# Chunked attention beside matrix products: five pieces per tile, or two turns per tile

## The chip, the cores and the metric

One core of one Trainium2 chip runs the whole program. The metric is the device time of one execution in microseconds (us); less is better. TensorE (PE) does the matrix products, VectorE (DVE), ScalarE (ACT) and GpSimd (POOL) work element by element, and SyncE (SP) issues most of the DMAs.

## The reference, cut to what matters

```python
# attention: 4 batches, 8 heads, 768 rows, 64 columns; chunks of 32 queries
for c in range(nc):
    k_full = concat(mem_k, k[16 rows before the chunk .. 8 rows after it])
    v_full = concat(mem_v, v[the same rows])
    scores = scale * q_c @ k_full.T
    a = exp(scores - max(scores)); a = a / (sum(a) + 1e-9)
    out[chunk] = a @ v_full
x = out as (3072, 512)
h = x @ w_in;  x = (h * tanh(softplus(h))) @ w_out
xn = x / rms(x) * rms_g
return (silu(xn @ w_gate) * (xn @ w_val)) @ w_out2
```

All inputs are float32. The kernel splits each operand of a large product into a high and a low part and adds three products of the parts.

## The kernel before, in words

The 3072 rows are worked in four batches of 768. A batch has six attention tiles of 128 rows (`TPP` is 6). The first batch's attention runs at the start. The attention of batch j (1, 2, 3) runs beside the products with `w_in` of batch j - 1, whose rows are then already there. For batch 1 these products are the units (`unit`, L682), for batches 2 and 3 the groups (`group1`, L714, over `group`, L643: seven products per group by a Strassen-like scheme). A product (`product`, L632) is six matmuls of 128x128 by 384 columns, recorded under L639, L640 and L641. Both `unit` and `group` yield after each product. The stretch from one yield to the next is called a slot. Batch 1 has 52 slots, batches 2 and 3 have 56 each.

At each yield `run` (L699) calls `between` (L998, made by `slots`, L990). It counts the slots in `n`, issues stores that are due, calls attention pieces until their share is done, converts some weights, and from slot `n_slots - 7` on builds the operands T of the next stage out of the new attention rows (`tail_of`, L1022, with its sums at L615 to L618 and splits at L153 and L154).

One attention tile t takes five operations on PE, each followed by work of other engines:

- a (L433): four 128x128 transposes of the queries (L438) and four of the next keys (L395), in one of two rotating PSUM banks each (`bank`, L332). It also issues the loads of later queries and keys. a1 (L445) copies them out on ACT (L449, L408, L409) and DVE (L404). `att_a0` does the first keys of a batch.
- b (L453): the scores, 32 small matmuls of a 64x32 block by 64 columns, into the bank pair `bkp` (L458). A small float32 matmul leaves two records. b1 (L466): DVE takes the maximum and subtracts it (L471, L472), ACT takes the exponential (L477).
- c (L486): four transposes of the probabilities (L490), into a rotating bank. c1 (L495) copies them on ACT (L497).
- d (L501): the values, again 32 small matmuls, into the same bank pair `bkp` (L506). It issues the load of the values of tile t + 2. d1 (L516): DVE forms the sums and multiplies (L519, L520, L522).
- e (L528): four transposes of the result (L532), into a rotating bank. e1 (L535) copies them on ACT (L539).

`att_list(j)` (L544) makes the list for a batch: step s holds e of tile s - 4, d of s - 3, c of s - 2, b of s - 1 and a of s, each with its own follow-up as one piece. That makes 31 pieces with the one of `att_a0`. `between` spreads them evenly: piece number m is called at the first slot n with `m * (n_slots - 7) < n * 31`.

The order in which each engine gets its instructions is set at build time by a planner (`schedule_with_timeline_sim`, L19). It goes by program order as priority, and may put an instruction ahead of, or behind, others if its model of the engines finds them not ready. `pin` keeps the order of some.

Of the kernel before, what the change touches and what calls it, by code (L numbers as in the profile page):

```python
# [29 lines left out]
def tile_kernel(  # L30
# [30 lines left out]
    TPP = 2 * NSUB  # L61
# [45 lines left out]
    def flush(all_=False):  # L107
        tick[0] += 1
        while late and (all_ or late[0][0] <= tick[0]):
            _, dst, src = late.pop(0)  # L110
            nc.sync.dma_start(out=dst, in_=src)
# [197 lines left out]
    def cv_upto(n):  # L309
        while cv_n[0] < n:  # L310
            next(cv[0], None)
            cv_n[0] += 1
# [231 lines left out]
    def att_list(j):  # L544

        out = []
        t0 = TPP * j
        for s in range(TPP + 4):
            for op, lag in (("e", 4), ("d", 3), ("c", 2), ("b", 1), ("a", 0)):
                t = t0 + s - lag  # L550
                if t0 <= t < t0 + TPP:
                    if op == "a" and t % SPB == 0:
                        out.append([(att_a0, t)])
                    out.append([(att_ops[op], t), (att_ops[op + "1"], t)])
        return out


    ttab_x, ttab_n = {}, {}

    def t_new():  # L560
# [2 lines left out]
    def g_new():  # L563
        return gp.tile([128, 2, N], F32, tag="g", name="g")
# [16 lines left out]
    def t_pieces(j, x0, x1, new, temp_new, dram, tab):  # L581

        return sum_pieces(j, x0[:, 0:2, :], x0[:, 2:4, :], x1[:, 0:2, :], x1[:, 2:4, :],
                          new, temp_new, dram, tab)
# [405 lines left out]
    def slots(pieces, conv, tail=(), more={}, cap=10 ** 6):  # L990


        state = dict(n=0, att=0, tail=0)
        plist, n_slots = pieces
        first_cv, to = conv
        base = cv_n[0]

        def between():  # L998
            state["n"] += 1
            n = state["n"]  # L1000
            flush()
            if n in more:
                more[n]()
            span = n_slots - 7
            while state["att"] < len(plist) and state["att"] * span < n * len(plist):
                for fn, t in plist[state["att"]]:
                    fn(t)
                state["att"] += 1
            if n > first_cv:
                cv_upto(min(cap, base + (to - base) * (n - first_cv) // (n_slots - first_cv)))  # L1010
            if n >= n_slots - 7 and tail:
                if state["tail"] == 0:
                    state["t"] = tail()
                    for fn in state["t"][0]:
                        fn()
                elif state["tail"] <= len(state["t"][1]):
                    state["t"][1][state["tail"] - 1]()
                state["tail"] += 1

        return between  # L1020

    def tail_of(j):  # L1022
        return lambda: t_pieces(j, xb.pop(2 * j), xb.pop(2 * j + 1), t_new, lambda p: g_new(), None, ttab_x)

    def keep_w(i, half):
        return lambda: w_store(("i", i), half)
# [5 lines left out]
    CV_I = 64  # L1032

    def then(more, n, fn):
        more.setdefault(n, []).append(fn)

    def finish_at(more, i, n):
        part = finish(("i", i))
        for step in range(3):
            then(more, n + step, lambda: next(part))  # L1040

    def calls(more):
        return {n: (lambda fns=fns: [fn() for fn in fns]) for n, fns in more.items()}

    units = [(1, i) for i in range(NHEAD)]
    units += [(b, i) for i in (3, 4, 7, 5, 6) for b in range(2)]
    at = {u: 4 * n + 4 for n, u in enumerate(units)}
    more = {}
    finish_at(more, 7, at[1, 7] + 1)
    bt = slots((att_list(1), 4 * len(units)), (0, 73), tail_of(1), calls(more), CV_I)  # L1050
    for b, i in units:
        run([unit(b, i)], bt)
    for i in range(3):
        del wtab["i", i]
    more = {}
# [4 lines left out]
        finish_at(more, i, 3 * n + 1)  # L1060
    for n, i in ((8, 2), (15, 1), (22, 0)):
        then(more, n, lambda: None)
    bt = slots((att_list(2), 56), (12, CV_I + 33 + 11), tail_of(2), calls(more), CV_I + 33)
    for i in down:
        group1(1, i, bt)
    more = {}
    for i, ns in ((0, (1, 3)), (1, (8, 10)), (2, (15, 17))):
        for half, n in enumerate(ns):
            then(more, n, keep_w(i, half))
    bt = slots((att_list(3), 56), (0, 0), tail_of(3), calls(more))  # L1070
    for pos, i in enumerate(up):
        group1(2, i, bt)
        reload(pos, up)
# [2 lines left out]
    def late_pool(name, bufs, side="left"):  # L1076
        return ctx.enter_context(tc.tile_pool(name=name, bufs=bufs, side=side, reuse_waits="tile"))
# [1 line left out]
    w2p[0] = late_pool("w2p", 1, "right")  # L1079
    late_pools["s"] = late_pool("gs", 3, "right")  # L1080
    late_pools["gr"] = late_pool("gr", 1, "right")
    bt = slots(([], 56), (0, CV_I + 44))
    for pos, i in enumerate(down[:-1]):
        group1(3, i, bt)
        if 1 <= pos <= 3:
# [41 lines left out]
    for s, (m, i) in enumerate(steps):  # L1127
        t = feed.next(s)
# [57 lines left out]
    def between2(to, n_slots):  # L1186
        state = dict(n=0)
        base = cv_n[0]

        def fn():  # L1190
            flush()
            if pend:
                pend.pop(0)()
                return
            n_raw[0] = 10 ** 6
            state["n"] += 1
            cv_upto(min(to, base + (to - base) * state["n"] // n_slots))

        return fn

    bt = between2(CV_I + 220, 100)
# [13 lines left out]
    units = [(j, r) for j in jback for r in range(NSUB2)]  # L1215
# [17 lines left out]
    bt = between2(CV_I + 298, 92)  # L1233
# [54 lines left out]
```

## Time and profile before

| what | us |
|---|---|
| median of 3 runs | 1166.82 |
| lowest and highest of them | 1164.63, 1167.36 |
| the profiled execution, its own time | 1167.72 |
| its span, from first to last instruction | 1166.0 |

In the timeline a row is a start, a duration, an engine and a line. Matmuls are pipelined, so a duration overlaps the next start. What an operation costs PE is read from the distance between starts. In rows of stretches, each engine has its busy time and its count of instructions, then follow the granted clock of PE as a share of full speed, the busy share of the DMA engines, and GB/s.

### The profile page before, as it was taken

The page shows a single profiled execution, that of the slowest core. Times are in us where ns is not written, and L with a number is a line of the kernel's source. Part 1 is how long each engine was busy: PE and PEld are TensorE (multiplying, and loading weights), DVE is VectorE, ACT ScalarE, POOL GpSimd, SP SyncE. Part 2 cuts the span into 40 slices and gives each one's busy share as a digit, 9 for nine tenths or more (in the row PEclk, how much of TensorE's full clock was granted, in tenths as well). Part 3 has the DMA queues.
Part 4 walks back from the last instruction along what each step waited for, and adds up shares of the span by engine and source line. Part 5 has one row for each costly group of instructions (what it writes and reads, how often), then busy time and mean ns, then how long its engine had stood idle before and what let it go on. Part 6 is the DMA issues. An engine that isn't in the chain of part 4 may idle for free.

```text
span 1166.0 us, 22910 instructions
## 1 busy us (share of the span) xinstructions
PE 1140.7 (98%) x9052; PEld 1005.2 (86%) x9052; DVE 823.8 (71%) x1254; ACT 629.2 (54%) x1008; POOL 183.4 (16%) x165
## 2 busy tenths in 40 slices
PE   5899999999999999999999999999999999999998
PEld 4799999999999888888878778888888888999998
DVE  3655798844745876866776765967896857888873
ACT  4566666543645896677775443544454423444441
POOL 3011231311132311010011121110211111000000
PEclk8899999999999999999999999999999999999999
DMA  9989799898488774594599398999898889655421
GB/s 195 187 219 224 191 300 260 240 297 284 170 302 290 255 225 144 188 354 157 195 375 409 123 349 316 355 407 359 312 363 356 329 283 319 180 160 145 145 91 37
DMA packets 213276, 294.20 MB, mean 252 GB/s; under 512 B 104240, under 2 KB 160560, under 8 KB 204336
## 3 DMA queue, kind: packets, MB, share of 16 engines
q1 hardware_dynamic: 210864, 284.34, 73.5%
q0 software_dynamic: 2304, 8.39, 2.3%
q8 instruction: 71, 1.16, 0.4%
q14 instruction: 37, 0.30, 0.1%
HBM read 181.80 MB, written 110.89 MB: 251 GB/s over the span
## 4 chain that ended last, share of the span: by engine, by line
PE 75%; DMA 9%; DVE 8%; ACT 5%; issue 2%; POOL 0%; SPq 0%; ACTq 0%; DVEq 0%; POOLq 0%
PE bk L639 13%; PE bk L640 13%; PE bk L641 13%; DMA s<-g_scratch 4%; PE bk L912 4%; PE bk L914 4%; PE bk L913 4%; PE bk L755 3%; PE bk L756 3%; PE bk L754 3%; DVE T L154 2%; PE bkp L639 2%; PE bkp L640 2%; PE bkp L641 2%; PE bkp L506 2%
## 5 line engine op out<-in xcount | busy, mean ns | idle before, releaser
L639 PE MATMUL bk<-T,w 128*128 128x384 f32 (+1 forms) x860 | 315.6, 369 | 1.3 <-ACT c L657 1.0
L640 PE MATMUL bk<-T,w 128*128 128x384 f32 (+1 forms) x860 | 311.2, 362 | 0.0
L641 PE MATMUL bk<-T,w 128*128 128x384 f32 (+1 forms) x860 | 307.4, 361 | 0.0
L639 PEld LDWEIGHTS bk<-T,w 128*128 128x128 f32 x860 | 162.0, 189 | 21.0 <-ACT c L657 1.3
L640 PEld LDWEIGHTS bk<-T,w 128*128 128x128 f32 x860 | 161.9, 188 | 16.5 <-DVE T L154 0.3
L641 PEld LDWEIGHTS bk<-T,w 128*128 128x128 f32 x860 | 161.5, 188 | 15.8
L912 PE MATMUL bk<-w,T 128*128 128x256 f32 x396 | 112.1, 283 | 0.2 <-ACT T L153 0.2
L913 PE MATMUL bk<-w,T 128*128 128x256 f32 x396 | 112.0, 283 | 0.0
L914 PE MATMUL bk<-w,T 128*128 128x256 f32 x396 | 111.9, 283 | 0.0
L755 PE MATMUL bk<-T,w 128*128 128x512 f32 x276 | 107.5, 390 | 0.5 <-DVE T L154 0.5
L756 PE MATMUL bk<-T,w 128*128 128x512 f32 x276 | 107.1, 389 | 0.0
L754 PE MATMUL bk<-T,w 128*128 128x512 f32 x276 | 105.8, 389 | 0.0
L669 POOL TENSOR_TENSOR v<-c,v 128x512 f32<-128x512 f32 x36 | 54.1, 1503 | 291.7 <-DVE c L665 259.0
L665 DVE TENSOR_TENSOR c<-bk,c 128x512 f32<-128x512 f32 (+2 forms) x72 | 43.0, 598 | 54.5 <-PE bk L641 41.9
L912 PEld LDWEIGHTS bk<-w,T 128*128 128x128 f32 x396 | 76.0, 192 | 0.5 <-ACT T L153 0.4
L913 PEld LDWEIGHTS bk<-w,T 128*128 128x128 f32 x396 | 76.0, 192 | 0.0
L914 PEld LDWEIGHTS bk<-w,T 128*128 128x128 f32 x396 | 75.9, 192 | 0.0
L649 ACT COPY c<-bk 128x512 f32<-128x512 f32 (+2 forms) x72 | 36.9, 514 | 69.1 <-PE bk L641 25.3
L154 DVE TENSOR_TENSOR T<-s,T 128x1024 fp32r<-128x1024 f32 (+1 forms) x50 | 62.5, 1258 | 15.2 <-ACT T L153 15.1
L782 ACT ACTIVATE s<-s 128x1024 f32<-128x1024 f32 x44 | 46.4, 1059 | 31.3 <-DMA s<-g_scratch 31.2
L755 PEld LDWEIGHTS bk<-T,w 128*128 128x128 f32 x276 | 51.8, 188 | 11.6 <-DVE T L154 0.9
L756 PEld LDWEIGHTS bk<-T,w 128*128 128x128 f32 x276 | 51.8, 188 | 10.8
(228 smaller groups left out, 2284.6 us busy)
## 6 DMA issues: line engine op xcount, KB each, us to landing
T<-nt_scratch SPq DMA_DIRECT2D x35, 1024.0 KB
g_scratch<-g SPq DMA_DIRECT2D x64, 384.0 KB
s<-g_scratch SPq DMA_DIRECT2D x46, 512.0 KB
h_scratch<-s SPq DMA_DIRECT2D x36, 512.0 KB
w<-wg SPq DMA_DIRECT2D x10, 1792.0 KB
wg<-w SPq DMA_DIRECT2D x30, 512.0 KB
raw<-in_moe_w_out_dram SPq DMA_DIRECT2D x28, 512.0 KB
nt_scratch<-T SPq DMA_DIRECT2D x14, 1024.0 KB
```

Of the source, the lines that this page charges most:

```text
L154: keep((eng or nc.vector).tensor_tensor(lo, src, hi.bitcast(F32), op=ALU.subtract))
L639: nc.tensor.matmul(ps, whi, xh, start=first and kk == 0, stop=False, **more)
L640: nc.tensor.matmul(ps, whi, xl, start=False, stop=False, **more)
L641: nc.tensor.matmul(ps, wlo, xh, start=False, stop=kk == 1, **more)
L669: nc.gpsimd.tensor_tensor(c22, u3, z5, op=ALU.add)
L754: nc.tensor.matmul(ps, ahi, bhi, start=start, stop=False)
L755: nc.tensor.matmul(ps, ahi, blo, start=False, stop=False)
L756: nc.tensor.matmul(ps, alo, bhi, start=False, stop=stop)
L782: nc.scalar.activation(x, g, self.act)
L912: nc.tensor.matmul(ps, t[:, 0, f], w[:, 0], start=first and f == 0, stop=False, **more)
L913: nc.tensor.matmul(ps, t[:, 0, f], w[:, 1], start=False, stop=False, **more)
L914: nc.tensor.matmul(ps, t[:, 1, f], w[:, 0], start=False, stop=f == HG - 1, **more)
```

## The change: two turns per tile

The list of pieces is replaced by a list of turns, each with a place on the axis of slots. For step s (0 to 8) the near turn holds b of tile s - 1, a of s, then a1 of s and b1 of s - 1. The far turn, 0.62 of a step later, holds d of s - 2, e of s - 3, c of s - 1, then d1 of s - 2, e1 of s - 3 and c1 of s - 1. A step is `span / 8.62` slots: 5.22 for batch 1 and 5.68 for batches 2 and 3. `att_list` stays in use for batch 0.

```diff
+    def att_turns(j, span):
+
+        t0 = TPP * j
+        out = [(0, [(att_a0, t0)])]
+        for s in range(TPP + 3):
+            near = [(att_b, s - 1), (att_a, s), (att_a1, s), (att_b1, s - 1)]
+            far = [(att_d, s - 2), (att_e, s - 3), (att_c, s - 1), (att_d1, s - 2), (att_e1, s - 3),
+                   (att_c1, s - 1)]
+            for at, ops in ((s, near), (s + 0.62, far)):
+                ops = [(fn, t0 + t) for fn, t in ops if 0 <= t < TPP]
+                if ops:
+                    out.append((at * span / (TPP + 2.62), ops))
+        return out
...
-        plist, n_slots = pieces
+        tiles, n_slots = pieces
+        plist = att_turns(tiles, n_slots - 7) if tiles is not None else []
...
-            span = n_slots - 7
-            while state["att"] < len(plist) and state["att"] * span < n * len(plist):
-                for fn, t in plist[state["att"]]:
+            while state["att"] < len(plist) and plist[state["att"]][0] < n:
+                for fn, t in plist[state["att"]][1]:
                     fn(t)
                 state["att"] += 1
...
-    bt = slots((att_list(1), 4 * len(units)), (0, 73), tail_of(1), calls(more), CV_I)
+    bt = slots((1, 4 * len(units)), (0, 73), tail_of(1), calls(more), CV_I)
...
-    bt = slots((att_list(2), 56), (12, CV_I + 33 + 11), tail_of(2), calls(more), CV_I + 33)
+    bt = slots((2, 56), (12, CV_I + 33 + 11), tail_of(2), calls(more), CV_I + 33)
...
-    bt = slots((att_list(3), 56), (0, 0), tail_of(3), calls(more))
+    bt = slots((3, 56), (0, 0), tail_of(3), calls(more))
...
-    bt = slots(([], 56), (0, CV_I + 44))
+    bt = slots((None, 56), (0, CV_I + 44))
```

## Rows read from the trace of the kernel before

**Rows 1.** The page, busy time of each engine.

```profile
PE 1140.7 (98%) x9052; PEld 1005.2 (86%) x9052; DVE 823.8 (71%) x1254; ACT 629.2 (54%) x1008; POOL 183.4 (16%) x165
```

**Rows 2.** Stretches: start:end, length, busy (count) PE, PEld, DVE, ACT, POOL; clock, DMA, GB/s.

```profile
140.00:180.00 40.00, 40.00 (x536) 36.83 (x535) 39.39 (x70) 27.59 (x54) 11.56 (x14) 1.00 0.97 284
...
226.00:300.10 74.10, 73.92 (x1148) 67.58 (x1147) 36.71 (x74) 29.67 (x57) 8.19 (x8) 1.00 0.87 274
300.10:365.00 64.90, 64.80 (x358) 62.34 (x357) 40.09 (x64) 36.10 (x60) 17.24 (x15) 1.00 0.76 268
```

**Rows 3.** Waits of PE from 60 to 345 us: total, times, longest.

```profile
PE bk L395 <- DVE kw L412: 0.9, 1, 0.9
PE bk L639 <- DVE c L665: 0.2, 1, 0.2
```

**Rows 4.** PE by line, 63.1 to 300.1 us; L641 as L640, L506 as L458.

```profile
L639 PE MATMUL bk<-T,w 128*128 128x384 f32 x319 | 113.0, 355 | 0.2 <-DVE c L665 0.2
L640 PE MATMUL bk<-T,w 128*128 128x384 f32 x318 | 107.9, 339 | 0.0
...
L458 PE MATMUL bkp<-kw,qT 64*32 64x64 f32 x1152 | 17.5, 224 | 0.0
...
L395 PE MATMUL bk<-ident,kn 128*128 128x128 f32 (+1 forms) x76 | 11.8, 266 | 0.0
L490 PE MATMUL bk<-ident,p 128*128 128x128 f32 x72 | 11.2, 278 | 0.0
```

**Rows 5.** Timeline of PE, a d and a c, each alone between products.

```profile
242.91 0.34 PE L641 MATMUL bk<-T,w 128*128 128x384 f32 x1
243.18 0.86 PE L506 MATMUL bkp<-vw,pT 64*32 64x65 f32 x64
...
244.26 0.34 PE L640 MATMUL bk<-T,w 128*128 128x384 f32 x1
...
244.95 0.34 PE L641 MATMUL bk<-T,w 128*128 128x384 f32 x1
...
245.75 0.33 PE L640 MATMUL bk<-T,w 128*128 128x384 f32 x1
245.92 0.33 PE L641 MATMUL bk<-T,w 128*128 128x384 f32 x1
...
247.48 0.34 PE L641 MATMUL bk<-T,w 128*128 128x384 f32 x1
```

**Rows 6.** Timeline of PE, a b with an e right behind it.

```profile
202.35 0.34 PE L641 MATMUL bk<-T,w 128*128 128x384 f32 x1
202.62 0.86 PE L458 MATMUL bkp<-kw,qT 64*32 64x64 f32 x64
203.41 0.66 PE L532 MATMUL bk<-ident,x 128*128 128x128 f32 x4
...
204.08 0.34 PE L640 MATMUL bk<-T,w 128*128 128x384 f32 x1
```

**Rows 7.** Timeline of PE, a b cut by products, first to last part.

```profile
145.21 0.34 PE L639 MATMUL bk<-T,w 128*128 128x384 f32 x1
145.48 0.41 PE L458 MATMUL bkp<-kw,qT 64*32 64x64 f32 x20
...
146.10 0.34 PE L641 MATMUL bk<-T,w 128*128 128x384 f32 x1
...
149.03 0.30 PE L458 MATMUL bkp<-kw,qT 64*32 64x64 f32 x4
```

**Rows 8.** Timeline, a b and a d, and the DVE steps that free `bkp`.

```profile
154.58 0.86 PE L458 MATMUL bkp<-kw,qT 64*32 64x64 f32 x64
...
161.01 0.68 DVE L472 TENSOR_TENSOR p<-bkp,mx 128x512 f32<-128x512 f32 x1
...
186.02 0.86 PE L506 MATMUL bkp<-vw,pT 64*32 64x65 f32 x64
...
189.84 0.68 DVE L522 TENSOR_TENSOR x<-bkp,sm 128x512 f32<-128x512 f32 x1
```

## The prediction

> **What bounds the kernel now.** I read the page first: PE is busy for 98% of the span [rows 1], so the question is what PE does, and whether it ever waits for the attention. The stretches come next. From 140 to 180 us, from 226 to 300 and from 300 to 365, PE is busy for practically all of the time at a granted clock of 1.00 [rows 2]. Then the waits: from 60 to 345 us, where the attention of batches 1 to 3 runs, PE waits only twice, 1.1 us together [rows 3]. So these stages are bound by PE issuing instructions one after the other. A change there can gain by making attention cheaper for PE, and can lose by making PE wait. What is saved passes on, because the stage behind is bound by PE too [rows 2]: its loads, conversions and stores are issued as products advance, so they move along.
>
> **What attention costs PE now.** Between 63.1 and 300.1 us PE does 319 + 318 + 318 = 955 matmuls of products, 1152 records each of scores and values, and 72 or 76 transposes of each of four kinds [rows 4]. One product matmul takes (247.48 - 245.92) / 9 = 0.1733 us from start to start [rows 5]. Thus 955 x 0.1733 = 165.5 us of the 237.0 are products, and 71.5 us are attention.
>
> What would it be if every operation stood alone and whole? A d alone moves a product from 242.91 to 244.26, which is 1.35 us, where two product steps take 0.35: so it costs 1.00 us [rows 5]. A c alone costs 245.75 - 244.95 - 0.35 = 0.45 us [rows 5]. There are 1152 / 64 = 18 b and 18 d, and (3 x 72 + 76) / 4 = 73 sets of four transposes: 36 x 1.00 + 73 x 0.45 = 68.9 us. The kernel pays 71.5, in spite of some neighbours that already save a little. The rest is in bursts cut in parts. One b is cut in four [rows 7]: the part of 20 records costs 146.10 - 145.21 - 0.35 = 0.54 us, where 20/64 of the 0.79 us that a whole burst occupies [rows 6] would be 0.25. A part too many so costs 0.29 us. In the timeline of the three batches I count nine such parts: three in each of the first b of batches 2 and 3, and three single ones. Those first b come right behind a (pieces 1 and 3 of the list, 3.2 slots apart at most), and the planner puts products between the parts that are ready.
>
> **The change, part by part.**
>
> *Neighbours.* A b with an e behind it costs 204.08 - 202.35 - 0.35 = 1.38 us [rows 6], against 1.00 + 0.45 apart: 0.07 saved by the contact of small matmuls with transposes. For contact between two sets of transposes I take nothing. Per batch, the near turns make five such contacts (b with a, s = 1 to 5) and the far turns six (d with e or c, s = 2 to 7). In three batches that is 33 x 0.07 = 2.3 us. Whole turns would cost 68.9 - 2.3 = 66.6 us, against 71.5: **4.9 us less**.
>
> *Cuts.* That sum has no part cut. Bounds: all nine cuts come back (2.6 us lost again) or none. The a of a tile now lies a whole step, 5.68 slots (5.22 in batch 1), ahead of its b, so the two b in four parts should become whole; the single cuts, where the planner fills a hole, can recur anywhere. I take two, 0.6 us.
>
> *The bank pair.* Scores and values share `bkp`, and the two turns are closer than the pieces were. From d to the next b the list had two pieces, 2 x 49/31 = 3.2 slots, with a c between; now there are 0.38 x 5.68 = 2.16 slots, with e and c. At 6 x 0.1733 = 1.04 us a slot that is 2.25 + 0.9 = 3.15 us. From b to the next d it was 4.7 slots; now 0.62 x 5.68 = 3.52 slots and a's 0.9 us, 4.6 us. What DVE needs, in the stretch where it is busy for 39.39 of 40 us [rows 2]: behind the b at 154.58 the subtraction ends at 161.69, 6.25 us after the burst's end; behind the d at 186.02 the multiplication ends at 190.52, 3.64 us after [rows 8]. At those lags PE would wait 1.65 and 0.5 us. From 226 us on DVE is half busy [rows 2], and I see no wait. Bounds: nothing (the planner puts the burst behind products when it expects the lag, as it does now: a lag of 6.25 us and no PE wait in that stretch [rows 3]), up to 6 x (1.65 + 0.5) = 12.9 us for batch 2, all six tiles at the worst rows. A gain is excluded, as there is next to nothing to remove. I am nearest to the row without waits, and take 0.3 us.
>
> *Other engines.* The work of DVE, ACT and POOL is the same in number and shape. In a near turn a1's copies (one on DVE, three on ACT) now stand ahead of b1; behind them wait c and then d, but c comes only after 4.6 us, d and e, and d a full step after c1. In a far turn d1 stands behind e on PE because `x` has one buffer, and e1 goes ahead of c1 on ACT. Each is covered by the slots to the next turn; if that cover goes, the price is the one of the bank pair. The two rotating banks are reused in the order q, k, e, c; between c and the next q lie 2.16 slots and a b, 3.2 us, for two copies on ACT, which is busy for 27.59 of 40 us [rows 2].
>
> *DMAs moved.* SP gets the same DMAs. The loads of v at d(t) are used at d(t + 2), two steps or 11.4 slots later, where the list had 11 at its closest; q likewise 11.4 against 7.9; the keys after a batch's first 5.68 against 4.7. PE waits for no DMA now [rows 3], and the closest distances grow, so I cost them at nothing. If a v load came late, the stores behind it on SP would be late too, and their buffers.
>
> *Ends of batches.* The last e comes at slot 49 (45 in batch 1), in the same call as the sums that need it and ahead of them, one slot later than in the list; but its d is now five slots ahead instead of 1.6, so its x is ready. I cost this at nothing: the seven slots up to the next stage hide the sums and splits, as they do now. If that cover went, the price would be the slot that it is later, 1.04 us.
>
> **Sum.** 4.9 - 0.6 - 0.3 = 4.0 us less: 1167.7 - 4.0 = 1163.7 us against the profiled execution. That lies 0.9 us above the median of the runs, so I predict **1162.8 us**. About 0.3%, 3.5 us, is what a measurement of this kernel can tell from no change, so this is just beyond it.
>
> **A rule against it.** Going from a product to a d takes 0.27 us instead of 0.17, in which the product behind has to drain [rows 5]. So what costs is a change between small and whole matmuls. The Trainium skill, page "TensorEngine Tiling (Array Packing)", section "Tiling Modes", says that changing the tiling mode, not just the tile, drains TensorE. By it, a b or d pays for entering and leaving whatever whole-array work stands beside it, and turns would save only what cuts cost. The row with the neighbour [rows 6] speaks against that, by 0.07 us only.
>
> **Rivals.**
>
> 1. *The planner takes the turns apart again.* It already shifts attention where its model sees holes. All nine cuts then come back, 2.6 us, and 4.9 - 2.6 = 2.3 us remain: 1164.5 us, the same within 0.3%. For it: cuts in all three batches now. Against: the worst ones come from a b too close behind its a. Chance 0.29.
> 2. *Only whole bursts count, contacts save nothing.* Then 2.6 us of cuts less the 0.6 and 0.3 above leave 1.7 us: 1165.1 us. Against it, the contact's row [rows 6]. Chance 0.09.
> 3. *`bkp` becomes the bound in batch 2.* PE stands in b or d until DVE has emptied the bank pair, and every product behind stands too, as PE works in order. At the worst rows, 12.9 - 4.9 = 8.0 us slower: 1174.8 us. It decides when the waits exceed 4.9 + 3.5 = 8.4 us, 0.7 us for each of batch 2's twelve b and d. For it: DVE is full from 140 to 180 us and the distances shrink. Against: the order is planned with the lag in view, and the first tiles, with the 6.25 us, now come later, where DVE has caught up more. Chance 0.14.
>
> **How the numbers follow.** My forecast holds 0.48, with a saving between 3.5 us and about 6 us (no cut, both present waits gone). Rivals 1 and 2 give the same within 0.3%, 0.38; rival 3 gives slower, 0.14. The range reaches from 1166.8 - 7.3 = 1159.5 us (all of it, with the spread of the runs) to 1169.0 us, which takes in rivals 1 and 2 and a mild form of rival 3 with some 2 us lost net; the rest of rival 3 and a little below are left out.
>
> **What would show it.** Right: from 60 to 300 us PE takes about 4 us less with the same counts, b and d stand as 64 records with transposes right behind, a set of b, q, k costs about 1.83 us, and the waits of PE stay below 2 us. Wrong: more than two parts of b or d with products between them, or PE waiting for L472 or L522, or for copies of ACT. The sum fails if the time saved by 300 us is lost again before the end, as waits for loads.

## The result, and the profile after

The changed kernel takes 1177.47 us (median of 6 runs), the kernel before 1167.09 us in the same session: a ratio of 1.0093, with a 95% interval of 1.0072 to 1.0114. It is slower by about 10 us, where 4 us less was forecast, and lies outside the range. The profiled execution took 1179.36 us, with a span of 1177.6 us, 11.6 us above that of before.

The page's first part, to be set beside [rows 1]: the same instructions on PE, 4 us more busy time, a longer span.

```profile
PE 1145.0 (97%) x9052; PEld 1008.1 (86%) x9052; DVE 827.6 (70%) x1254; ACT 628.8 (53%) x1008; POOL 182.1 (15%) x165
```

The waits of PE, from 60 to 360 us (total, times, longest), answer to [rows 3]: 7.7 us where there were 1.1. None is a wait of b (L458) or d (L506) for DVE. Product lines are 14 higher in this kernel: L653 is L639.

```profile
PE bk L653 <- ACT w L153: 3.2, 2, 2.8
PE bk L395 <- DMA kn<-in_k_dram: 1.4, 1, 1.4
PE bk L438 <- DMA qn<-in_q_dram: 1.1, 1, 1.1
PE bk L653 <- DVE g L682: 1.1, 1, 1.1
PE bk L395 <- DVE kw L412: 0.9, 1, 0.9
```

Where was the time lost? Product matmuls come in the same number in both kernels, so I counted them in both timelines and compared the start of the same one. A product also starts later when more attention happens to lie ahead of it. The last column takes that off, at 1.00 us for a whole b or d and 0.45 us for a set of four transposes.

```
place (stage, slot)          before    after    difference   without attention ahead
units, first                   44.4     44.9       0.5          0.5
units, slot 36 of 64          101.8    100.9      -0.9          0.6
units, slot 54                127.7    130.2       2.6          1.1
units, slot 58                134.7    142.2       7.5          6.6
products of batch 1, slot 2   145.0    153.0       8.0          7.0
the same, slot 50 of 56       217.0    224.0       7.0          7.0
products of batch 2, slot 0   225.0    235.6      10.6          8.7
the same, slot 20             256.0    264.9       8.8         10.3
the same, slot 30             271.0    282.7      11.6         11.2
the same, slot 50             300.9    311.4      10.4         10.4
products of batch 3, slot 54  375.0    385.7      10.7         10.7
```

So the loss lies in three places: 5.5 us at the last units, 3.3 us from the end of the stage after them to slot 20 of the next, and 0.9 us in the ten slots behind that, of which 0.8 us come back by slot 50. From there to 386 us little is lost or won after that; the last 0.9 us came later, and I didn't follow them.

The first place, in the timeline of PE. After a far turn, PE stands for 2.76 us until ACT has made the high part of the last units' weights. Behind the wait the products start 0.32 us apart instead of 0.17.

```profile
132.57 0.86 PE L506 MATMUL bkp<-vw,pT 64*32 64x65 f32 x64
133.36 0.66 PE L532 MATMUL bk<-ident,x 128*128 128x128 f32 x4
136.77 0.69 PE L653 MATMUL bk<-T,w 128*128 128x384 f32 x1 [2.76 <-ACT w L153]
137.26 0.52 PE L654 MATMUL bk<-T,w 128*128 128x384 f32 x1
137.58 0.52 PE L653 MATMUL bk<-T,w 128*128 128x384 f32 x1
```

The stretches there (columns as in [rows 2]) show why: the granted clock is 0.53 from 137 to 143 us, that is, mostly the lower of its two levels, 1.2 GHz. In 6 us, in which PE was busy throughout, this costs an estimated 6.0 x 0.47 = 2.8 us more, as much as the wait.

```profile
130.00:137.00 7.00, 4.24 (x85) 3.66 (x84) 6.48 (x11) 3.66 (x8) 3.00 (x4) 0.92 0.80 183
137.00:143.00 6.00, 6.00 (x23) 5.91 (x24) 3.93 (x8) 3.35 (x7) 1.88 (x2) 0.53 0.79 209
```

Why were the weights late? They go half by half through ACT and DVE (L202, L205, L209, L210, L216, L153). Timeline of DVE in the kernel before, the tenth and eleventh halves (L210), with one step of the attention pieces between them:

```profile
93.04 0.69 DVE L210 SCALAR_TENSOR_TENSOR ca<-raw,ca 128x512 int32<-128x512 int32 x1
...
96.44 0.69 DVE L522 TENSOR_TENSOR x<-bkp,sm 128x512 f32<-128x512 f32 x1
...
97.69 0.69 DVE L210 SCALAR_TENSOR_TENSOR ca<-raw,ca 128x512 int32<-128x512 int32 x1
```

The same two halves in the changed kernel: a near turn and a far turn come between them, and 4.7 us have become 11.1.

```profile
89.88 0.69 DVE L210 SCALAR_TENSOR_TENSOR ca<-raw,ca 128x512 int32<-128x512 int32 x1
92.99 0.69 DVE L471 TENSOR_REDUCE mx<-bkp 128x8 f32<-128x512 f32 x1 [2.42 <-PE bkp L458]
...
94.36 0.68 DVE L216 CUSTOM_DVE_ANT_0 ca<-ca,lr 128x1024 uint16<-128x1024 uint16 x1
...
99.24 0.69 DVE L522 TENSOR_TENSOR x<-bkp,sm 128x512 f32<-128x512 f32 x1
...
100.99 0.69 DVE L210 SCALAR_TENSOR_TENSOR ca<-raw,ca 128x512 int32<-128x512 int32 x1
```

DVE has idle time there: the conversion wasn't short of an engine, its next step (L216) stood behind attention (L471) in the engine's order. The 3.3 us of lateness stayed, and grew. The split that PE waits for is the one at 136.10, of the fifteenth half; in the kernel before it came at 131.88 and ended 0.13 us before the first product that uses it. From the timelines of ACT and PE, first before, then after:

```profile
131.88 0.62 ACT L153 CAST w<-ca 128x512 fp32r<-128x512 f32 x1
132.63 0.44 PE L639 MATMUL bk<-T,w 128*128 128x384 f32 x1
```

```profile
136.10 0.62 ACT L153 CAST w<-ca 128x512 fp32r<-128x512 f32 x1 [2.54 <-DVE ca L216]
```

Some 1.3 us of these 4.2 us have another origin. On DVE two subtractions of the weights of column pair 7 stand ahead of L216 of this half. They took 1.29 us before, while POOL rested, and take 2.56 us here, beside POOL's copies of memory rows of v. Timelines of DVE and POOL, first before, then after:

```profile
127.54 1.29 DVE L154 TENSOR_TENSOR w<-sm,w 128x768 fp32r<-128x768 f32 x2
```

```profile
132.81 0.87 POOL L385 COPY vw<-vw 8x780 f32<-8x780 f32 x1 [1.63 <-DMA vw<-in_mem_v_dram]
132.90 2.56 DVE L154 TENSOR_TENSOR w<-sm,w 128x768 fp32r<-128x768 f32 x2
134.23 0.96 POOL L385 COPY vw<-vw 8x780 f32<-8x780 f32 x1 [0.56 <-PE bk L532]
135.39 0.68 DVE L216 CUSTOM_DVE_ANT_0 ca<-ca,lr 128x1024 uint16<-128x1024 uint16 x1
```

Elsewhere in this trace an L154 of 128x768 takes 0.95 us while POOL rests (92 of them, none over 0.97); the one here took 1.59 us. No run keeps these two engines apart, so the share of 1.3 us is an estimate.

The second place, end of the next stage, in SP's own timeline: two batches meet here, and v loads and their memory rows fill SP's queue until 228.8 us. Only then are keys issued.

```profile
226.52 2.20 SPq L379 DMA_DIRECT2D vw<-in_v_dram  x4
228.83 0.35 SPq L111 DMA_DIRECT2D g_scratch<-g  x1
229.28 1.21 SPq L344 DMA_DIRECT2D kn<-in_k_dram  x2
```

PE has the transposes of these keys ahead of its products, as the planner pulled them forward: the program calls them at slot 6 of the next stage, and PE has them two slots before that stage starts. From issue to use they have 4.0 us; in the kernel before it was 11 us (221.95 to 233.0). PE stands 1.38 us for them, and soon after 1.14 us for a bank:

```profile
231.10 0.76 PE L458 MATMUL bkp<-kw,qT 64*32 64x64 f32 x52
233.23 0.63 PE L395 MATMUL bk<-ident,kn 128*128 128x128 f32 x4 [1.38 <-DMA kn<-in_k_dram]
...
238.13 0.44 PE L653 MATMUL bk<-T,w 128*128 128x384 f32 x1 [1.14 <-DVE g L682]
```

The third place: queries are issued right behind a load and a store of weights (1.8 MB and 0.9 MB), and land when PE already stands. SP first, then PE:

```profile
266.92 0.35 SPq L127 DMA_DIRECT2D w<-wi  x1
267.31 1.05 SPq L132 DMA_DIRECT2D wi<-w  x1
268.45 0.55 SPq L358 DMA_DIRECT2D qn<-in_q_dram  x1
```

```profile
281.31 0.63 PE L438 MATMUL bk<-ident,qn 128*128 128x128 f32 x4 [1.15 <-DMA qn<-in_q_dram]
```

And the saving? From 63.62 to 311.54 us PE does 960 product matmuls and the attention of the three batches. The kernel before does the same work from 63.20 to 301.10 us. First after, then before:

```profile
L653 PE MATMUL bk<-T,w 128*128 128x384 f32 x320 | 113.0, 354 | 4.4 <-ACT w L153 3.2 <-DVE g L682 1.1
```

```profile
L639 PE MATMUL bk<-T,w 128*128 128x384 f32 x320 | 113.4, 355 | 0.2 <-DVE c L665 0.2
```

Products take 960 x 0.1733 = 166.4 us in either. After, 247.9 - 166.4 = 81.5 us are left; less 6.9 us of waits (the one for L412 lies ahead of this stretch) and 2.8 us of clock, that is 71.8 us for attention. Before, it is 237.9 - 166.4 - 0.2 = 71.3 us. The attention itself became no cheaper.

In the order of PE's instructions, batch 0's leftovers included, contacts of small matmuls with transposes rose from 33 to 55. The b in parts by products were 5 + 27, 10 + 11 + 9 + 2, 12 + 12 + 8, 2 + 30 and 2 + 30 of 32 matmuls before. Now they are 5 + 27, 18 + 8 + 6, 6 + 26 and 13 + 10 + 5 + 2 + 2. That is eight parts too many in either kernel (of the prediction's nine, one is cut off by transposes, not by products).

### The profile page after: what moved, and what is told of

It is laid out like the page before. It is cut to its first block, busy times and chain, and to the rows that moved or that the text cites. A ratio compares the mean times of both kernels' runs of the same rounds, so it can differ in the third digit from the quotient of the medians.

```text
span 1177.6 us, 22914 instructions
## 1 busy us (share of the span) xinstructions
PE 1145.0 (97%) x9052; PEld 1008.1 (86%) x9052; DVE 827.6 (70%) x1254; ACT 628.8 (53%) x1008; POOL 182.1 (15%) x165
## 4 chain that ended last, share of the span: by engine, by line
PE 76%; DMA 8%; DVE 7%; ACT 5%; issue 2%; POOL 1%; SPq 0%; ACTq 0%; DVEq 0%; POOLq 0%
PE bk L653 13%; PE bk L654 13%; PE bk L655 12%; PE bk L926 4%; PE bk L928 4%; PE bk L927 4%; DMA s<-g_scratch 3%; PE bk L769 3%; PE bk L770 3%; PE bk L768 3%; PE bkp L653 2%; PE bkp L654 2%; PE bkp L655 2%; DMA qn<-in_q_dram 1%; DVE T L154 1%
## 5 line engine op out<-in xcount | busy, mean ns | idle before, releaser
L653 PE MATMUL bk<-T,w 128*128 128x384 f32 (+1 forms) x860 | 315.3, 369 | 5.3 <-ACT w L153 3.2
L653 PEld LDWEIGHTS bk<-T,w 128*128 128x128 f32 x860 | 162.9, 190 | 24.8 <-ACT w L153 3.8
L154 DVE TENSOR_TENSOR T<-s,T 128x1024 fp32r<-128x1024 f32 (+1 forms) x50 | 61.8, 1243 | 17.1 <-ACT T L153 17.0
```

What stands on the lines that cost most here:

```text
L154: keep((eng or nc.vector).tensor_tensor(lo, src, hi.bitcast(F32), op=ALU.subtract))
L653: nc.tensor.matmul(ps, whi, xh, start=first and kk == 0, stop=False, **more)
```

## The experiments

Theory A: PE works in order, and the turns make particular inputs late: weights beside the units, keys and queries in SP's row. Rival B: every tile of two turns loses a little. Later came rival R: the old order was planned around inputs that arrive just in time, and any new plan loses some us somewhere, turns or not. Ratios are to runs of the kernel before on the same chip, with 95% intervals; "places" are those of the table above.

### Turns in some batches only

```diff
+    TURNS = (1,)        # e1;  (2, 3) in e2
-        plist = att_turns(tiles, n_slots - 7) if tiles is not None else []
+        plist = (att_turns if tiles in TURNS else att_old)(tiles, n_slots - 7) if tiles is not None else []
```

Here `att_old` gives the old list at its old places.

> Turns only beside the units (batch 1), the old list in batches 2 and 3. Theory A (late inputs: PE stands in order for weights, keys and queries that come later than planned; the wait for the last units' weights and the half clock behind it are worth some 6 us): 5 to 8 us slower than before, with a wait of PE for the ACT split of w near 134 us. Rival B (every tile of two turns loses a little, wherever it stands, by cuts and by the bank pair): a third of the loss, 3 to 4 us slower, and no such wait.

> Turns only in batches 2 and 3, the old list beside the units. Theory A: no wait for w near 134 us; what is left are the waits for keys and queries, 2 to 5 us slower than before. Rival B: two thirds of the loss, 7 us slower.

Batch 1 alone: 1.0047 (1.0031 to 1.0062). The wait is there (L153, 2.8 us), the difference stands at 5.1 us at slot 58 of the units (attention ahead taken off), and it is the same at slot 50 of batch 2's products. Batches 2 and 3 alone: 1.0067 (1.0054 to 1.0081), more than A expected and near the 7 us of B. But there is no wait for w near 134 us, and at most 1 us is lost in the units; then come waits for queries (2.0 us), weights (1.4 us) and a bank (0.6 us). From slot 50 of batch 1's products to slot 50 of batch 2's, 5.9 us are lost: these waits, and an estimated 1.7 us of clock behind the one for queries (0.72 over 6 us). So the losses sit at waits, as A says, and not evenly in the tiles, which speaks against B; but A had the size of those in batches 2 and 3 too small.

### The completion of weights moved, keys and queries off SP's row

```diff
-    finish_at(more, 7, at[1, 7] + 1)
+    finish_at(more, 7, at[1, 7] + 9)
```

> All turns, but the completion of the weights of column pair 7 (two sums, POOL, two splits) is called eight slots later, beside the last unit. Theory A1 (it stands ahead of the last conversion on DVE and ACT and makes that late): the wait of 2.8 us for w and the half clock go, 5 to 7 us faster than the changed kernel, about 1171 us. Rival A2 (the turns' own work on DVE and ACT, or the late load of the raw weights, delays the conversion): within 2 us of the changed kernel, 1175 to 1179 us, wait still there.

1.0056 (1.0038 to 1.0074). The wait of 2.8 us is gone, but one of 1.4 us for the same kind of split stands at 141.5 us; the loss at the last units shrinks by some 4 us and new waits (for v, for L472) appear later. Half of A1.

```diff
-        nc.sync.dma_start(out=qt, in_=q[b, ...
+        (nc.gpsimd if t > 7 else nc.sync).dma_start(out=qt, in_=q[b, ...
-            nc.sync.dma_start(out=t, in_=k[b, :, s0:s0 + 128, :]...
+            (nc.gpsimd if b > 0 else nc.sync).dma_start(out=t, in_=k[b, :, s0:s0 + 128, :]...
```

> All turns, but the keys and queries of batches 1 to 3 are loaded from POOL's queue, past SP's row of v loads and weight stores. Theory A (keys and queries wait in SP's row): the waits of PE for keys (1.4 us) and queries (1.1 us) go, 2 to 4 us faster than the changed kernel, about 1174 us. Rival (the transfers themselves are slow, the DMA engines being busy): the waits stay, within 1 us of the changed kernel.

1.006 (1.004 to 1.008), as A expected: the waits for keys and queries are gone from the list, the one for w is not.

```profile
PE bk L653 <- ACT w L153: 3.2, 2, 2.8
PE bk L395 <- DVE kw L412: 0.9, 1, 0.9
PE bk L653 <- ACT g L741: 0.8, 1, 0.8
PE bk L532 <- DVE x L522: 0.6, 1, 0.6
```

The difference to before grows by 3.4 us from slot 50 of batch 1's products to slot 50 of batch 2's in the changed kernel; here it stays (6.8 and 6.7 us, attention ahead taken off). For the query this bears out SP's row as the cause: POOL issues it at 260.13 us, 8.3 us earlier than SP did, and PE uses it at 277.70 us without a wait. For the keys it doesn't. POOL issues them only 1.4 us earlier, but in this plan PE has their transposes 8.7 us later. First POOL, then PE:

```profile
227.88 0.90 POOL L344 DMA_DIRECT2D kn<-in_k_dram  x1
```

```profile
241.89 0.66 PE L395 MATMUL bk<-ident,kn 128*128 128x128 f32 x4
```

### Attention kept in its place

```diff
+    def hold(ins):
+        return pin(ins) if held[0] else ins
...
-            nc.tensor.matmul(
+            hold(nc.tensor.matmul(
```

The same for all of PE's attention instructions, in the changed kernel (e5), in the kernel before (e6), and with both other edits (e9).

> All turns, with PE's attention instructions of batches 1 to 3 kept behind the products traced before them, so that the planner can't put them ahead of their turn. Theory A (the planner pulls attention ahead of its turn, where its inputs are late and where bursts get cut): parts too many fall from eight to three (some 1.5 us), the waits of PE for keys and queries (2.5 us) go; the wait for w beside the units stays; 3 to 6 us faster than the changed kernel, 1172 to 1174 us. Rival (pulling ahead fills holes that PE would otherwise wait in): new waits of PE at the starts of stages, no faster than the changed kernel.

> The kernel before (list of pieces) with PE's attention instructions kept behind the products traced before them. Theory A: parts too many fall from eight to two, no wait is added; 1 to 2 us faster than before or the same. Rival (holes): slower than before by 1 us or more, with new waits at the starts of stages.

> Turns held in place as in e5_hold_turns, keys and queries from POOL's queue as in e4_kq_pool, conversions called faster as in e7_conv84. Theory A: all three causes are gone, what remains is what the turns save: 1163 to 1167 us, the same as before or up to 0.3% faster. Rival (the turns themselves cost PE or DVE something that no wait shows): still 3 us or more slower than before.

Theory A's part on the planner falls. Held turns: 1.0203 (1.0177 to 1.0229); held list: 1.007 (1.0046 to 1.0093); all edits: 1.0159 (1.0137 to 1.0181). Parts too many did fall to four and two in the first two, and no wait for keys or queries was left. But products now wait in their place for weights that attention used to cover. The waits of held turns:

```profile
PE bk L658 <- ACT w L153: 10.5, 5, 5.7
PE bkp L511 <- DMA vw<-in_v_dram: 2.1, 1, 2.1
PE bk L660 <- DVE w L154: 1.9, 2, 1.4
```

What the planner pulls ahead fills holes in front of late weights; cuts are the price of that, and a small one.

### Conversions called earlier

```diff
-    bt = slots((1, 4 * len(units)), (0, 73), tail_of(1), calls(more), CV_I)
+    bt = slots((1, 4 * len(units)), (0, 84), tail_of(1), calls(more), CV_I)
```

With turns everywhere (e7), with the list (i1), and with turns in batch 1 only (i2).

> All turns, with the conversions beside the units called faster (their place ends at step 84 instead of 73, still capped at 64). Theory A1b (the last units' weights are called too late for turns): the wait of 2.8 us for w and the half clock behind it go, 4 to 7 us faster than the changed kernel, 1171 to 1173 us. Rival (the raw loads of 512 KB, one behind the other through two buffers, set the time of the conversion, not the place of the call): wait still there, 1176 to 1179 us.

> The kernel before (list), with the conversions beside the units called faster (84 instead of 73, capped at 64). No turns. If the earlier conversions themselves, or any new plan, cause the loss behind the units that e7_conv84 showed: 3 to 10 us slower than before, lost between 140 and 240 us. If that loss is the turns': the same as before within 2 us.

> Turns beside the units only, with the same faster conversions; the list in batches 2 and 3. If what e1_turns_batch1 lost (5.5 us) is the late weights alone: no wait for w near 134 us, and at the end of the units 1 to 2 us ahead of before; in total as i1_list_conv84 less 1 to 2 us. If it is the turns as such: 4 us or more behind at the end of the units.

e7: 1.0127 (1.0097 to 1.0157). The wait for w beside the units is gone, as A1b said, and yet the kernel is slower. With attention ahead taken off, 2.6 us are lost where the next stage begins, 4.3 us in its course and 6.4 us at its end. i1: 1.0042 (1.0024 to 1.006), without any turn: 2.2 us are lost at the same first place, so that loss isn't the turns'. i2: 1.0053 (1.0036 to 1.0071): 2.4 us there, and 5.2 us more in the course of that stage, where i1 loses 0.6 us; that I didn't follow. But at the end of the units (slot 62) i2 stands at -0.9 us, from 0.6 at their start. Of this 1.6 us, 0.9 us are two sets of transposes that the kernel before has ahead of that product and i2 has behind it. So 0.7 us are gained over before. i1, with the same conversions and the same attention ahead, stands at 0.8 us. From 60 to 142 us i2's PE has one wait:

```profile
PE bk L395 <- DVE kw L412: 0.9, 1, 0.9
```

So the loss at the last units is the late weights. Without it turns beside the units are worth 0.7 us over the kernel before, and some 1.6 us over i1. At the end of the stage in e7 PE waits for weights in four places, 3.5 us together; why they are late there I can't explain.

### Controls without turns

```diff
-            while state["att"] < len(plist) and state["att"] * span < n * len(plist):
+            while state["att"] < len(plist) and (state["att"] + 0.5) * span < n * len(plist):
```

Minus 0.5 in h1; g3 is the list with the queue of e4.

> The kernel before (list of five pieces per tile), every piece called half a piece (0.8 slot) later. A control with no turns in it. Theory A (turns make particular inputs late): same as before within 3 us, no wait for w above 1 us. Theory R (the order was planned around inputs that come just in time, and any new plan loses several us in some place, turns or not): 3 to 9 us slower than before, with waits of PE for w, T, or banks at other places.

> The kernel before (list of five pieces per tile), every piece called half a piece (0.8 slot) earlier. Control without turns. Theory R (any new plan loses several us by inputs that come just in time): 3 to 12 us slower than before, with new waits of PE. Theory A (only turns make inputs late): within 3 us of before.

> The kernel before, with the keys and queries of batches 1 to 3 from POOL's queue. No turns. Theory A: no wait for them to remove, the same as before within 2 us. Theory R: 3 us or more slower by new waits.

Later by half a piece: 1.0054 (1.0031 to 1.0077); earlier: 1.0046 (1.0025 to 1.0066); the other queue: 1.0014 (1.0001 to 1.0027). R holds for the two shifts: they lose half of what the turns lose. It fails for g3, where it had 3 us or more and A had at most 2: not every new plan loses. g1's waits are spread over many causes:

```profile
PE bk L532 <- DVE x L522: 1.7, 1, 1.7
PE bk L639 <- DVE c L665: 1.3, 3, 0.5
PE bk L640 <- issue: 1.0, 1, 1.0
```

### Mending the turns

> All turns, keys and queries from POOL's queue, conversions beside the units called a little faster (78 instead of 73, capped at 64). Theory A: the waits for w at the last units (6 us with the half clock) and for keys and queries (3 to 4 us) go, 1166 to 1170 us. Theory R: one wait goes and another comes, 1172 us or more.

> All turns, with both edits that helped alone: keys and queries from POOL's queue (3 us) and the weights of pair 7 completed eight slots later (2 to 3 us). Theory A: they add, 1170 to 1173 us. Theory R: they don't add, 1174 us or more.

> As g2_turns_pool_conv78 (1170.7 us), and the first and last keys of a batch too come from POOL's queue. If the wait for keys of 1.1 us near 236 us comes from SP's row: it goes, 1 us faster, 1168 to 1170 us. If the transfers are slow: still there, 1170 to 1172 us.

g2 has e4's queue and 78 in place of 84: 1.0026 (1.0007 to 1.0044), the best with turns in all three batches, at 1170.65 us. It lies between A and R: most of the loss is mended, some 3 us stay in smaller waits (1.6 us for w, 1.1 for keys, 1.0 for a bank, 1.0 for w's low part). g4, e3 and e4 together: 1.0033 (1.0015 to 1.0051); the two edits add. h4 moves the remaining key loads too, and is worse, 1.0056 (1.0034 to 1.0078): the wait for keys is still there, 1.6 us. In h4 POOL issues these keys only at 231.72 us, behind its own copies of memory rows (L385), and PE has their transposes at 238.07; in g2 it is 228.54 and 235.91. So POOL's queue had them hardly earlier than SP's (229.28 in the changed kernel), or later, and 6 to 7 us from issue to use weren't enough.

> Turns only in batch 3, the list in batches 1 and 2, all loads from SP. Theory A and R alike: nothing changes up to about 225 us; then the turns save some 2 us where no wait is added, and the wait for a query load (1 to 2 us, with up to 1 us of disorder) comes back near 280 us: 1 us faster to 2 us slower than before. If batch 3 loses 5 us or more, the loss there is not in the waits that I named.

> Turns only in batch 3, keys and queries from POOL's queue. If the late query load is what spoils batch 3: no wait there, 1 to 3 us faster than the list with the same queue (g3_list_pool, 1168.8 us), so 1166 to 1168 us. If not: slower than g3_list_pool.

Turns in batch 3 alone, where DVE is half busy: 1.0004 (0.9981 to 1.0028) and, with the other queue, 1.0009 (0.999 to 1.0028), the same as before. In h2 the query load is in time, and a v load is late instead, by 2.32 us; in its profiled execution batch 3 loses 4.3 us, though the runs as a whole are level. h3 has no new wait beyond 0.3 us, and from the start of batch 3's attention (2.0 us behind, a difference of the run's first 45 us for the greater part) to its end (1.9 us) it gains 0.1 us. That is the turns' own worth there over the kernel before. No variant beat the kernel before.

## Why the prediction was wrong, step by step

- *What bounds the kernel* was right: PE in order, and the time lost by slot 50 of batch 2's products is still there at 386 us. But I read the near absence of waits [rows 3] as room. It was the sign of the contrary, inputs that came just in time. The split for the last units ended at 132.50 us before, and the first product that uses it started at 132.63 us; nothing in my text asked how much slack was behind a wait of zero.
- *Neighbours* isn't borne out. There are 22 contacts more, which at 0.07 us would be 1.5 us (the 2.3 us counted contacts that partly existed). But attention cost 71.8 us against 71.3, so the sum shows nothing of it; what took it up I can't place. The 0.7 us of batch 1 (i2) and the 0.1 us of batch 3 (h3) are what turns gained where their inputs were in time.
- *Cuts*, **"the two b in four parts should become whole"**, failed. The first b of batch 2 has three parts. The first of batch 3 became whole, but now the second there is in five; eight parts are too many as before. The step took the distance in the program, 5.68 slots, for one on PE. The planner pulled b of batch 2's first tile to the start of its stage, where the program calls it at slot 6, and cut it there. Rival 1 had this, with its consequence of 2.3 us gain as an upper end.
- *The bank pair* cost nothing: no wait of b or d for DVE in the changed kernel. Rival 3 had the sign, but its place and its mechanism were wrong.
- *Other engines*, **"each is covered by the slots to the next turn"**, is the step that failed most. I followed what waits inside the attention, and not what is queued behind it on DVE and ACT: the conversion of weights. It was delayed by 4.2 us at the split that PE waits for (some 1.3 us of it by subtractions that ran slower beside POOL), and cost a wait of 2.8 us and 2.8 us of lower clock.
- *DMAs moved*, **"I cost them at nothing"**, failed in the second and third places (1.4 and 1.1 us of direct waits). The distances in slots had grown in the program. But the query stood in SP's row behind weight traffic whose slots are fixed, which e4 bears out, and the keys had 4.0 us from issue to use instead of 11, as the planner pulled their use forward and v loads filled SP's row where two batches meet.
- *Ends of batches* cost nothing that I could find.
- The sum that would have been right is: no saving, waits 7.7 - 1.1 = 6.6 us, clock 2.8 and the run's start 0.5: 9.9 of the 10.4 us at slot 50 of batch 2's products. The rest isn't placed.
- *A rule against it*: whether contacts save what [rows 6] said is not shown either way, and the loss came from waits, not from changes between small and whole matmuls.

How much of the loss is the turns'? The four controls without turns lose 0.14%, 0.42%, 0.46% and 0.54%. The wait for the weights is caused by turns beside the units: it comes with them (e1) and goes when the conversions are called earlier (i2), at another cost. That half of the loss could have struck any new plan is an inference from four controls, not shown.

## What to carry to other kernels

Where an engine in order shows no waits in a kernel planned ahead, look at what arrives just before it is used, and follow a moved step to the work queued behind it on every engine and DMA row, also the work of other stages. Price a reordering first by a control that shifts the order without the intended change: here two such controls lost 5 to 6 us, more than the whole gain at stake. Distances in program order say little where a planner may move instructions.

## What was unexpected in the hardware

A wait of PE of under 3 us can cost as much again in clock. In the changed kernel the wait of 2.76 us is followed by a clock of 0.53 over 6 us, 2.8 us more. In e1 the same wait of 2.76 us is followed by 0.72 over 6 us, 1.7 us more. In h2 a wait of 2.32 us for a v load falls in a stretch of 8 us at 0.79, 1.7 us more too. First e1, then h2:

```profile
136.00:142.00 6.00, 5.64 (x26) 5.55 (x27) 4.92 (x8) 3.92 (x8) 1.90 (x2) 0.72 0.81 221
```

```profile
270.00:278.00 8.00, 5.68 (x74) 5.17 (x73) 1.46 (x5) 1.06 (x2) 0.00 (x0) 0.79 0.81 224
```

Behind a wait of 1.60 us in g2, and behind one of 2.10 us in e5 (from 288.5 us), the clock stayed at 1.00. First g2, then e5:

```profile
141.00:147.00 6.00, 5.56 (x44) 5.19 (x44) 6.00 (x7) 4.92 (x10) 3.28 (x5) 1.00 0.95 214
```

```profile
290.00:298.00 8.00, 7.38 (x153) 6.61 (x154) 1.80 (x5) 2.04 (x4) 0.00 (x0) 1.00 0.82 236
```

In e2 a wait of 1.99 us was followed by 0.72 over 6 us. So the length of a wait didn't settle what it cost in clock, and these runs don't show what did. In the changed kernel the one wait of 2.8 us cost more than the three of 1.1 to 1.4 us, 3.7 us together: around those (226 to 250 and 276 to 286 us) the clock stayed at 1.00.
